# A transformer block on one core: an earlier start of the tensor engine, and instruction order set by hand dependencies

## The chip, the cores and the metric

The kernel runs on one core of one Trainium2 chip. The metric is device time in microseconds (us), as a median over runs. All runs quoted are of one core, and each run lists the mean clock granted to the tensor engine.

The engines go by the profile's names. PE is TensorE (matmuls), PEld its weight loads, DVE is VectorE, ACT is ScalarE, POOL is GpSimd and SP is SyncE. Two words need care. "The head" is the start of the kernel, up to the first q matmuls; "head 1" is `b_head` of chunk 1, the output projection described below. To evict is to copy a result out of PE's accumulator, which frees it for the next matmuls.

## The reference

The block has a pre-layernorm mixer and a gated MLP, S = 2048 rows, D = 1024. Cut to what matters:

```python
x = A_x
h  = x + A(layernorm(x))      # qkv = x @ wqkv; 32 heads of 32; each row attends to 8 rows,
                              # 0, 2, ..., 14 rows back (softmax over 8 logits); then @ wo
h2 = h + B(layernorm(h))      # z = gelu(x @ w_in); z1, z2 = halves of z; z2 = layernorm(z2)
                              # g = w_sp @ z2 + b_sp; (z1 * g) @ w_out
```

## The kernel before

The rows are worked in four chunks of 512. For each chunk there are four kinds of work, and they overlap across chunks:

1. `qkv(c)`: layernorm of x, transposes, then 192 matmuls on PE, evicted by ACT.
2. `attention(c)`: products and sums on DVE, about 80 us per chunk. For each of the 8 window positions `w`, DVE makes `part`, and four small PE matmuls write the logits `L`. After the eighth, softmax: DVE takes the maximum, ACT the exp, DVE the normalized `attn`. PE then spreads `attn` over the heads (`pb`), ACT evicts it (`AB`), and DVE makes the output `oT`.
3. `b_head(c)`: `oT @ wo` on PE, evicted by ACT (`hb`, `hnc`), then layernorm (`hnc` normalized by ACT).
4. `b_z2(c)`, `b_z1(c)`: the MLP's input matmuls, evicted by ACT with gelu (`u`, `z1s`).

```python
for i in range(NT):                       # layernorm of x, tile by tile
    xt = xts[i]
    st = l1.tile([P, 2, 6], FP32, name="bnst", tag="bnst")
    V.bn_stats(st[:, 0, :], xt[:, 0:512])
    V.bn_stats(st[:, 1, :], xt[:, 512:1024])
    V.bn_aggr(mv1[:, i, :], st[:])
    ...                                    # sqrt on ACT, reciprocal and normalize on DVE
    if c < 2:
        transpose_tile(...)                # 8 PE transposes, eviction by ACT
    ...
# attention(c)
for w in range(W_WIN):
    ...                                    # DVE: prod, t1_, t2_, part
    with tc.high_priority():
        for sq in range(4):
            T.matmul(L[32 * sq:32 * sq + 32, w, :], E32, part[:, sq * P:(sq + 1) * P], ...)
...
with tc.high_priority():
    A.activation(e, Ls, ACTF.Exp, scale=SCALE)
...
# program order
qkv(0); qkv(1); attention(0); qkv(2); b_head(0); attention(1); qkv(3); ...; b_head(1)
# then per chunk: b_z2(c), b_head(c+1) for c>0, b_z1(c), attention(c+2)
```

Each engine runs its instructions in the order that the build fixed (the traces of the changed kernel and of e4, two builds with the same order, agree in it on PE, DVE, ACT and POOL). A scheduler of the build works that order out from the program, its priorities and its own estimate of time. A "NoSync" dependency is there to change only this order, without a semaphore (a signal for which an engine waits).

## Time and profile before

| | |
|---|---|
| time | 773.97 us, median of 5 (773.35 to 774.67) |
| span of the profiled run | 772.2 us |
| PE busy | 742.4 us, 96% |
| first q matmul | 15.08 us |
| PE time lost after that | about 26 us (sum of what matmul starts lie further apart than usual), nearly all before 360 us |

From the profile page, the busy time of the engines (us, share of the span, instructions):

```profile
PE 742.4 (96%) x3704; PEld 379.9 (49%) x3704; DVE 439.6 (57%) x452; ACT 234.8 (30%) x304; POOL 20.1 (3%) x31
```

PE is the engine that bounds the kernel, so only moments when PE waits or runs slowly matter. The view of waits for PE names them. Its columns are: who waited, for whom, us in total, number of waits, the longest.

```profile
PE tpa L115 <- DVE xn L149: 9.8, 1, 9.8
PE L L229 <- DVE part L226: 4.8, 9, 2.0
PE acc L359 <- ACT u L361: 4.2, 1, 4.2
PE pb L253 <- DVE attn L245: 2.6, 3, 1.0
```

The first row is the start. The second is logits waiting for DVE's `part`. The third is a z2 matmul that finds no free accumulator, because ACT has not evicted one with gelu. The fourth is `pb` waiting for softmax.

The timeline of PE at the start (columns: start us, length us, engine, line, what; xN merges N instructions; in brackets, idle time before and what ended it):

```profile
9.83 4.15 PE L115 MATMUL tpa<-csb,xn 128*128 128x128 bf16 x32 [9.83 <-DVE xn L149]
15.08 5.21 PE L192 MATMUL acc<-xnT,wq 128*128 128x512 bf16 x14 [1.10 <-ACT xnT L116]
20.57 1.47 PE L192 MATMUL acc<-xnT,wq 128*128 128x512 bf16 x6
```

Fourteen q matmuls take 5.21 us, while six a little later take 1.47 us. Single starts show 0.425 us from one to the next for the first ten and 0.216 us after that: the array runs at half clock until about 19.2 us. The clock row of the page does not show it. It reads 9 (90% or more) from the first slice, because the first clock record of the trace, at 19.21 us, is the release itself.

The timeline of ACT around the 4.2 us wait:

```profile
245.02 4.62 ACT L328 ACTIVATE hnc<-hb,l2nb,l2rstd 128x1024 bf16<-128x1024 bf16 x4
249.66 1.28 ACT L239 ACT_TABLE_LOAD   x1
250.95 1.06 ACT L239 ACTIVATE scq<-scq 128x1024 bf16<-128x1024 f32 x1
252.02 1.28 ACT L361 ACT_TABLE_LOAD   x1
253.32 1.02 ACT L361 ACTIVATE u<-acc 128x1024 bf16<-128x1024 f32 x1
```

PE needs the gelu that starts at 253.32. Ahead of it in ACT's fixed order stand four normalizes (4.62 us) and exp of chunk 2 with a table load on each side (3.66 us together). The windows view gives what the wait does to the clock. Its columns are: window, length, then busy us (instructions) by engine, PEclk (1.00 is full), DMA share and GB/s.

```profile
237.00:250.00 13.00, 12.80 (x76) 6.38 (x75) 11.24 (x15) 12.82 (x15) 1.76 (x2) 1.00 0.37 122
250.00:262.00 12.00, 7.06 (x36) 3.87 (x34) 7.21 (x5) 9.43 (x13) 0.00 (x0) 0.72 0.58 135
```

A mean clock of 0.72 over 12 us is about 6.7 us at half clock (12 x 0.28 / 0.5). The clock record in the trace file has 6.83 us of it, from 254.73 us on.

### The profile page before, as it was taken

What the parts mean: (1) busy time and instruction counts of PE and PEld (TensorE: products, weight loads), DVE (VectorE), ACT (ScalarE), POOL (GpSimd) and SP (SyncE); (2) the same over time, 40 slices, a digit from 0 to 9 for tenths busy, and PEclk for the clock granted to TensorE, in tenths of its full rate; (3) what the DMA queues carried; (4) which work ended last, traced back from release to release, by engine and by line L of the source; (5) the groups of instructions that cost most, each with busy time, mean ns of one, the idle gap of its engine ahead of it and who ended that gap; (6) DMA issues with size and microseconds to landing.
All of it is one profiled execution on the core that took longest, in us unless ns stands there. A gap on an engine that the chain in (4) does not pass through costs nothing.

```text
span 772.2 us, 8881 instructions
## 1 busy us (share of the span) xinstructions
PE 742.4 (96%) x3704; PEld 379.9 (49%) x3704; DVE 439.6 (57%) x452; ACT 234.8 (30%) x304; POOL 20.1 (3%) x31
## 2 busy tenths in 40 slices
PE   4999999999999799999999999999999999999997
PEld 2666666546644444444545444444444444444443
DVE  6769799989998799979736020222222222212221
ACT  3522442256248845676551462000000000000000
POOL 0000000000000000000003000000000000000000
PEclk9999999999999899999999999999999999999999
DMA  9934364164884333145036957616211621020001
GB/s 330 340 132 97 124 180 138 56 225 112 291 304 165 66 134 115 41 178 124 14 141 250 276 191 215 190 31 175 71 42 42 178 68 42 28 81 28 1 21 62
DMA packets 104904, 102.24 MB, mean 132 GB/s; under 512 B 59232, under 2 KB 83200, under 8 KB 104736
## 3 DMA queue, kind: packets, MB, share of 16 engines
q1 hardware_dynamic: 98736, 75.52, 31.7%
q0 software_dynamic: 6128, 26.15, 9.8%
q8 instruction: 29, 0.48, 0.3%
q14 instruction: 11, 0.09, 0.0%
HBM read 55.19 MB, written 32.83 MB: 114 GB/s over the span
## 4 chain that ended last, share of the span: by engine, by line
PE 66%; DVE 23%; ACT 5%; issue 4%; DMA 1%; SPq 0%; DVEq 0%; ACTq 0%
PE acc L465 25%; PE acc L482 12%; PE acc L389 9%; PE acc L359 8%; PE acc L192 7%; DVE oT L264 5%; DVE prod L263 5%; DVE prod L220 4%; PE acc L303 4%; DVE scq L222 3%; DVE scq L224 2%; ACT hnc L328 1%; DVE part L226 1%; PE acc L490 1%; ACT AB L254 1%
## 5 line engine op out<-in xcount | busy, mean ns | idle before, releaser
L465 PE MATMUL acc<-wspT,z2sb 128*128 128x512 bf16 x896 | 194.0, 379 | 0.0
L465 PEld LDWEIGHTS <-z2sb 128*128 128x128 bf16 x896 | 87.7, 98 | 105.7
L468 DVE TENSOR_TENSOR g<-acc,bB 128x1024 bf16<-128x1024 f32 x28 | 34.3, 1225 | 159.7 <-PE acc L465 134.5
L359 PE MATMUL acc<-win,hnT 128*128 128x512 bf16 (+1 forms) x512 | 101.9, 358 | 4.2 <-ACT u L361 4.2
L389 PE MATMUL acc<-hnT,win 128*128 128x512 bf16 x448 | 98.8, 379 | 1.1 <-ACT z1s L392 1.1
L220 DVE TENSOR_TENSOR prod<-qT,kT 128x4096 bf16<-128x4096 bf16 x32 | 73.1, 2285 | 5.4 <-ACT kT L196 5.3
L359 PEld LDWEIGHTS <-hnT 128*128 128x128 bf16 x512 | 49.9, 99 | 50.8 <-issue 5.8
L389 PEld LDWEIGHTS <-win 128*128 128x128 bf16 x448 | 43.5, 98 | 52.1 <-issue 1.3
L482 PEld LDWEIGHTS <-zg 128*128 128x128 bf16 x420 | 41.1, 98 | 49.6
L263 DVE TENSOR_TENSOR prod<-vT,AB 128x4096 bf16<-128x4096 bf16 x28 | 64.1, 2291 | 1.4
L264 DVE TENSOR_TENSOR oT<-oT,prod 128x4096 bf16<-128x4096 bf16 x28 | 64.2, 2292 | 0.9
L192 PE MATMUL acc<-xnT,wq 128*128 128x512 bf16 x256 | 60.1, 389 | 2.0 <-ACT xnT L116 1.1
L199 ACT CAST stg<-acc 128x1024 bf16<-128x1024 f32 x36 | 36.2, 1013 | 79.9 <-PE acc L192 79.8
L303 PE MATMUL acc<-wo_sb,oT 128*128 128x512 bf16 x256 | 59.5, 379 | 0.0
L484 DVE TENSOR_TENSOR ot<-acc,hr 128x1024 bf16<-128x1024 f32 x15 | 18.4, 1224 | 69.4 <-PE acc L482 69.4
L192 PE MATMUL acc<-xnT,wv 128*128 128x512 bf16 x256 | 57.7, 380 | 0.0
L192 PE MATMUL acc<-xnT,wk 128*128 128x512 bf16 x256 | 56.8, 380 | 0.0
L482 PE MATMUL acc<-wout_a,zg 128*128 128x512 bf16 x240 | 54.2, 379 | 0.0
L192 PEld LDWEIGHTS <-wq 128*128 128x128 bf16 x256 | 36.1, 145 | 21.1 <-issue 4.8
L192 PEld LDWEIGHTS <-wk 128*128 128x128 bf16 x256 | 36.5, 144 | 18.2
L192 PEld LDWEIGHTS <-wv 128*128 128x128 bf16 x256 | 36.1, 144 | 17.5
L392 ACT ACTIVATE z1s<-acc 128x1024 bf16<-128x1024 f32 x28 | 28.4, 1025 | 42.6 <-PE acc L389 35.3
(97 smaller groups left out, 536.7 us busy)
## 6 DMA issues: line engine op xcount, KB each, us to landing
qkv_d<-stg SPq DMA_DIRECT2D x36, 256.0 KB, 2.9
z_d<-z1s SPq DMA_DIRECT2D x28, 256.0 KB, 2.9
z1c<-z_d SPq DMA_DIRECT2D x28, 256.0 KB, 2.7
z_d<-u SPq DMA_DIRECT2D x12, 448.0 KB, 3.6
z2sb<-z_d POOLq DMA_DIRECT2D x12, 448.0 KB, 8.5
xt<-in_A_x_dram SPq DMA_DIRECT2D x16, 256.0 KB, 9.7
xr<-in_A_x_dram SPq DMA_DIRECT2D x16, 256.0 KB, 2.8
h_d<-hb SPq DMA_DIRECT2D x16, 256.0 KB, 2.7
```

Source lines behind the costliest of these rows:

```text
L192: T.matmul(acc[:, j, :], wv[:, kt, dl, :], xnT[c][:, kt, :], start=(kt == 0), stop=(kt == KT - 1))
L199: A.copy(stg[:], acc[:])
L220: V.tensor_tensor(prod[:], qT[:], kT[:, :, o:o + CH], op=ALU.mult)
L263: V.tensor_tensor(prod[:], vT[:, :, o:o + CH], abb, op=ALU.mult)
L264: V.tensor_tensor(oT[:], oT[:], prod[:], op=ALU.add)
L303: T.matmul(acc[:, nh, :], oT[:, dl, il * P:(il + 1) * P], wo_sb[:, dl, nh * CH:(nh + 1) * CH], start=(last and dl == 0), stop=(dl == DLO - 1))
L359: T.matmul(accf[:, n0:n1], hnT[:, il, kt, :], wt[:, kt, n0:n1], start=(kt == 0), stop=(kt == KT - 1))
L389: T.matmul(acc[:, j, :].rearrange("p (a b) -> p a b", a=TPC), wt[:, kt, f0 * P:(f0 + 1) * P], hnT[:, :, kt, :], start=(kt == 0), stop=(kt ...
L392: A.activation(z1s[:], acc[:], ACTF.Gelu_apprx_tanh)
L465: T.matmul(acc[:, j, :], z2sb[a][:, f * P:(f + 1) * P], wspT[:, a, :], start=(a == 0), stop=(a == NT - 1))
L468: V.tensor_tensor(g1[:], acc[:], bB[:, c * CH:(c + 1) * CH].unsqueeze(1).to_broadcast([P, 2, CH]), op=ALU.add)
L482: T.matmul(acc[:, nh, :], zg[:, f, il * P:(il + 1) * P], wt[:, f0, nh * CH:(nh + 1) * CH], start=(f == 0), stop=(f == NF - 1))
```

## The change

The change has four parts.

1. **An earlier start.** The four x tiles of chunk 0 are requested first, on two queues. wq comes in eight pieces and is used as they come. The statistics of tile 3 move from DVE to ACT. The diff also takes the square roots of chunks 1 to 3 once per chunk instead of once per tile, evicts the transposes of tile 2 by DVE, and loads the table for the square root ahead.
2. **A warm clock.** Eighteen dummy matmuls on zeros keep PE busy from 1 us on, and ten more stand between and behind the transposes.
3. **Placement of logits** (`LATE`). For chunks 1 to 3, the first logits matmul of each window position may not stand before a named matmul in PE's order, so that PE does not stop for `part`.
4. **Placement of exp.** Exp of chunk 2 may not stand before a named gelu in ACT's order, the first one of the third row tile of z2 of chunk 0.

The diff, cut to its core:

```diff
+NWARM = 18
-    dma(csb[:], consts_d.ap()[:, :])
+    dma_w(csb[:], consts_d.ap()[:, :])
+    warm = cpool.tile([P, CH], BF16, name="warm")
+    V.memset(warm[:], 0.0)
 ...
+    wps = ps_att.tile([P, CH], FP32, name="wps", tag="L")
+    for _ in range(NWARM):
+        T.matmul(wps[:], warm[:, 0:P], warm[:], start=True, stop=True)
+    for i in (0, 3, 1, 2):
+        xts[i] = l1.tile([P, D], BF16, name="xt", tag="x2k", bufs=8)
+        (dma if i < 2 else A.dma_start)(xts[i][:], x2d[i * P:(i + 1) * P, :])
 ...
+    for kt in range(KT):
+        dma(wsb[0][:, kt, :], wq_view[:, kt, 0:D])
 ...
+    def stats_act(i):                      # tile 3: sums by two ACT passes
+        A.activation(jk[:], xts[i][:], ACTF.Identity, accum_out=sm[:, 0:1])
+        A.activation(jk[:], xts[i][:], ACTF.Square, accum_out=sm[:, 1:2])
 ...
+    def xpose(i, xn):
+        ... 8 transposes ...
+        for d in range(4 if i == 2 else 2):
+            T.matmul(wps[:], ident, xn[:, (d % 2) * CH:(d % 2 + 1) * CH], start=True, stop=True)
 ...                                        # q of chunk 0: four accumulators, kt outermost
+    LATE = {(1, 0): ('qkv', 2, 2, 0, 2), (1, 1): ('qkv', 2, 2, 2, 5), ... 24 entries ...}
 ...
+                    if sq == 0 and LATE.get((c, w)) in mms:
+                        tc.add_manual_dep(lg.ins, mms[LATE[c, w]].ins.name, <NoSync>, ...)
 ...
+        if c == 2:
+            tc.add_manual_dep(ex.ins, gelu[0, 2, 0].ins.name, <NoSync>,
+                              reason="exp of chunk 2 behind three gelu")
```

## The prediction

> **What bounds it now.** The tensor engine. The page has PE busy 742.4 of 772.2 us; the timeline shows back-to-back 512-column matmuls starting every 0.216 us, and that from 360 us on there is hardly a gap. The change touches only the first 350 us, so I count the time PE loses there (start-to-start distance above the normal one, read off the PE timeline):
> - Head: the first q matmul starts at 15.08 us, and its first ten run at 0.425 us each, about 2.2 us lost. The page's clock row does not show this (its records begin later). The Trainium skill ("TensorE: Matmul & The Clock Gate", Part 1) says the array clock is halved by default and released after some 3.4 us of sustained work; this trace agrees (fast from about 19.2 us).
> - Logits of chunks 1 to 3 waiting for VectorE's `part` (PE's waits): 2.1 us at 134, 1.2 at 215.5, 0.7 at 302, and some ten of 0.15 to 0.35: about 5.5 in sum.
> - At 249.9 us: 4.4 us waiting for ScalarE's gelu `u`. The ACT timeline shows why: four `hnc` (4.6 us), then exp of chunk 2 between two table loads of 1.28 us each, ahead of the gelu. The clock record then drops to half, and matmuls run at 0.425 us until 261: 2.3 us more, plus a 1.1 us wait for `attn`.
> - Left untouched: chunk 0's logits (2.4), `attn`, `stg` and `z1s` waits (4.5), the end (about 4).
>
> **What the change does.**
> - Head: x tiles are requested first and on two queues, wq comes in eight pieces used kt-first, one tile's statistics (about 1.6 us of VectorE) move to ScalarE (two 1.0 us passes). Tile 1 was waited for 1.0 us, until 6.06. The last normalize, at 12.9 now, should end near 10.3; transposes and eviction follow in about 2 us: first q matmul near 12.3 (gain 2 to 3.5). Eighteen dummy matmuls warm the clock meanwhile (gain 2.2); they cost nothing, PE being idle. Estimated from durations in this trace: 5.0 us, all critical, since PE has work from then on.
> - Logits placed some 5 to 9 matmuls (1 to 2 us) later for chunks 1 and 2: gain 2.2 + 1.4. VectorE continues meanwhile; three `part` buffers allow it.
> - Exp of chunk 2 behind three gelus: the gelu can follow `hnc` at 249.7, so the stall shrinks from 4.4 to about 1 us and the clock stays up: gain about 6. Exp comes some 5 us later, and attention of chunk 2 with it. That is off the critical path: oT of chunk 3 ends at 382 and is used at 399.4, a slack of 17 us, of which some 9 to 12 is consumed. Chunk 3's logits move some 8 us in the PE queue to match: gain 1.4.
>
> Sum: 5.0 + 3.6 + 6.0 + 1.4 = 16.0 us.
>
> **Prediction:** 758.0 us, 80% range 753.5 to 763.5. It sits near the 2% line (758.5): faster 0.53, same 0.46, slower 0.01.
>
> **What would show it.** Timeline: first q matmul at 11.5 to 13.2 us, at 0.216 us pitch from the start. PE's waits: `part` under 1.5 us in sum; the wait for `u` near 250 about 1 us or less, and no half-clock stretch after it. The order on ACT: gelu, gelu, gelu, exp. PE idle before the `wo` matmuls of chunk 3: none. PE busy time unchanged but for the dummies, and everything after 360 us only shifted.
>
> **What would make it wrong.** The clock falls again in the sparse stretch between dummies and q matmuls (minus 2). wq pieces or the x tiles land late. PE, now ahead, meets waits of VectorE elsewhere (oT of chunk 1 has only about 5 us slack; `attn`): the logits gain merely moves. ScalarE's deferred exp with its two table loads stalls a later gelu.

## The result, and the profile after

The changed kernel takes 760.52 us (median of 8, 759.62 to 761.81), against 773.55 us for the kernel before (median of 15). The ratio is 0.9835, 95% interval 0.9824 to 0.9846. Here and below, a ratio is the mean time of one kernel's fast runs over that of the other's in the same rounds, so it is not quite the ratio of the medians. The kernel is 1.65% faster: inside the predicted range, and inside 2%.

The eight runs fall into two groups: four at a mean clock of 1.000 take 759.62 to 760.02 us, and four at 0.997 or 0.998 take 761.01 to 761.81. The profiled run is of the first group (760.02), and that of the kernel before is a long one (774.33). So differences of about 1 us between medians of different kernels below can come from how many runs lost some clock; where that matters, runs at 1.000 are compared.

From the page of the changed kernel, the busy times, and then its view of PE's waits (columns as above):

```profile
PE 744.2 (98%) x3732; PEld 379.9 (50%) x3732; DVE 437.7 (58%) x445; ACT 236.3 (31%) x301; POOL 20.7 (3%) x32
```

```profile
PE L L288 <- DVE part L285: 3.3, 4, 2.2
PE pb L320 <- DVE attn L312: 2.7, 3, 1.0
PE tpa L170 <- DVE xn L162: 1.7, 1, 1.7
```

PE is busy 98% of a shorter span. The wait for gelu is gone from the list. The wait for `part` is not: 3.3 us remain in four waits, and the longest has grown from 2.0 to 2.2 us. It now sits elsewhere. The PE timeline of the start, and of the place where it sits:

```profile
11.81 0.61 PE L170 MATMUL tpa<-csb,xn 128*128 128x128 bf16 x8
13.30 7.10 PE L240 MATMUL acc<-xnT,wq 128*128 128x512 bf16 x32
...
209.28 2.75 PE L370 MATMUL acc<-wo_sb,oT 128*128 128x512 bf16 x12
214.20 0.24 PE L288 MATMUL L<-part,csb 128*32 128x128 bf16 x4 [2.17 <-DVE part L285]
```

The q matmuls start at 13.30 us at full speed: 32 in 7.10 us. At 214.20 us PE has waited 2.17 us for the first logits of chunk 2.

The ACT timeline of the changed kernel, and then its windows view where the kernel before had a clock of 0.72 (columns as above):

```profile
237.82 4.62 ACT L395 ACTIVATE hnc<-hb,l2nb,l2rstd 128x1024 bf16<-128x1024 bf16 x4
242.36 1.68 ACT L435 ACTIVATE junk<-u 128x1792 bf16<-128x1792 bf16 x1
244.03 1.00 ACT L428 ACTIVATE u<-acc 128x1024 bf16<-128x1024 f32 x1
245.03 0.79 ACT L428 ACTIVATE u<-acc 128x768 bf16<-128x768 f32 x1
245.81 1.01 ACT L428 ACTIVATE u<-acc 128x1024 bf16<-128x1024 f32 x1
248.22 1.06 ACT L302 ACTIVATE scq<-scq 128x1024 bf16<-128x1024 f32 x1
```

```profile
250.00:262.00 12.00, 11.03 (x80) 6.30 (x79) 10.14 (x7) 11.88 (x17) 0.00 (x0) 1.00 0.48 88
```

The three gelus (244.03, 245.03, 245.81) stand ahead of exp, and the clock is full. Exp is not late, though: it starts at 248.22 us, while before it started at 250.95.

To see where each us was won, I took the start of named matmuls from the two traces. The lead is by how much the changed kernel is ahead of the kernel before at that matmul:

| matmul | before, us | changed, us | lead, us |
|---|---|---|---|
| first q of chunk 0 | 15.08 | 13.30 | 1.78 |
| first v of chunk 0 | 46.94 | 43.30 | 3.64 |
| first matmul of head 1 | 215.03 | 208.85 | 6.18 |
| first logits of chunk 2 | 216.89 | 214.20 | 2.69 |
| first z2 of chunk 0 | 233.07 | 228.01 | 5.07 |
| first z2 of chunk 1 | 292.88 | 280.92 | 11.97 |
| first spatial matmul | 477.26 | 463.71 | 13.55 |
| end of span | 772.18 | 758.24 | 13.94 |

The lead falls between the third row and the fifth. A lead gained by PE was lost again at the logits of chunk 2, which DVE had ready only 2.69 us earlier than before.

### The profile page after: what moved, and what is told of

It is laid out like the page before. It is cut to its first block, busy times and chain, and to the rows that moved or that the text cites. A ratio compares the mean times of both kernels' runs of the same rounds, so it can differ in the third digit from the quotient of the medians.

```text
span 758.2 us, 8920 instructions
## 1 busy us (share of the span) xinstructions
PE 744.2 (98%) x3732; PEld 379.9 (50%) x3732; DVE 437.7 (58%) x445; ACT 236.3 (31%) x301; POOL 20.7 (3%) x32
## 4 chain that ended last, share of the span: by engine, by line
PE 63%; DVE 28%; ACT 4%; issue 4%; DMA 1%; DVEq 0%; ACTq 0%
PE acc L532 26%; PE acc L549 12%; PE acc L456 7%; PE acc L426 7%; DVE oT L331 6%; DVE prod L330 6%; PE acc L248 5%; DVE prod L279 5%; DVE scq L281 4%; PE acc L370 3%; DVE scq L283 2%; DVE part L285 1%; PE acc L240 1%; DVE oT L327 1%; PE acc L557 1%
## 5 line engine op out<-in xcount | busy, mean ns | idle before, releaser
L426 PE MATMUL acc<-win,hnT 128*128 128x512 bf16 (+1 forms) x512 | 98.9, 353 | 0.0
L248 PE MATMUL acc<-xnT,wq 128*128 128x512 bf16 x224 | 50.9, 380 | 0.0
L549 PE MATMUL acc<-wout_b,zg 128*128 128x512 bf16 x180 | 41.3, 379 | 0.0
```

The lines of the kernel that those rows point to most:

```text
L248: mms['qkv', c, xi, dl, kt] = T.matmul(acc[:, j, :], wv[:, kt, dl, :], xnT[c][:, kt, :], start=(kt == 0), stop=(kt == KT - 1))
L426: mms['z2', c, il, hf, kt, n0] = T.matmul(accf[:, n0:n1], hnT[:, il, kt, :], wt[:, kt, n0:n1], start=(kt == 0), stop=(kt == KT - 1))
L549: T.matmul(acc[:, nh, :], zg[:, f, il * P:(il + 1) * P], wt[:, f0, nh * CH:(nh + 1) * CH], start=(f == 0), stop=(f == NF - 1))
```

## The experiments

The comparison of instruction orders raised the first question. With the exp dependency and all eight placements of chunk 2 removed, the build gives the same instructions in the same order, on all engines, as the changed kernel. The traces (after, and e4 below) agree: PE 3732, DVE 445, ACT 301 and POOL 32 instructions, none at another place.

So part 4 and a third of part 3 change nothing in the presence of the rest. Two theories were set against each other. *Shared effect*: the reorder on ACT that removes the stall near 250 us follows from the placement of chunk 1's logits already, and the direct gain of that placement is partly lost at chunk 2. *Own shares*: each part brings what the prediction gave it.

### e1: the head alone

```diff
-    LATE = {(1, 0): ('qkv', 2, 2, 0, 2), ...}
+    LATE = {}
-        if c == 2:
+        if False:
             tc.add_manual_dep(ex.ins, gelu[0, 2, 0].ins.name, ...)
```

> The changed kernel without its placement table and without the exp dependency: only the new head is left. Head theory (both theories): every milestone of the before kernel from the k projection on comes 3.65 us earlier and nothing else changes; the 4.4 us stall near 246 us and the half-clock stretch are still there. About 770.0 us (ratio 0.995).

Measured: 770.5 us, ratio 0.9966 (0.9952 to 0.9981). The lead is 3.06 us at v of chunk 0 and 3.07 at the first spatial matmul: nothing else is gained. It is 0.6 us less than in the changed kernel, of which 0.5 us is a longer wait of PE at the transposes of chunk 1, near 25.1 us. The PE waits show the old stall unchanged:

```profile
PE L L288 <- DVE part L285: 4.8, 9, 2.0
PE acc L426 <- ACT u L428: 4.2, 1, 4.2
```

### e2: head and exp dependency, no placements

```diff
-    LATE = {(1, 0): ('qkv', 2, 2, 0, 2), ...}
+    LATE = {}
```

> Head plus the exp dependency, no placement table at all. Shared-effect theory: the ScalarE queue has exp of chunk 2 behind three gelus, as in the changed kernel, so the stall near 246 us and the half clock vanish: about 6.5 us below head only, 763.5 us. The 2.1 us wait of chunk 1's first logits (near 132 us) is back, but the 2.3 us wait of chunk 2's first logits (at 211.7 in the changed kernel) shrinks to about 1.2, so that PE arrives at z2 of chunk 0 within 1.2 us of the changed kernel. Rival (each part of the change brings its own share, as the prediction summed): also about 764, but PE would arrive at z2 of chunk 0 3.6 us later than in a kernel with the logits placed.

Measured: 764.46 us, ratio 0.9889 (0.9872 to 0.9906). The exp dependency by itself does bring the gelus ahead and is worth 6.5 us (lead 3.42 at z2 of chunk 0, 9.88 at z2 of chunk 1). Without placements, PE reaches z2 of chunk 0 with a lead of 3.42 us, 1.65 less than the changed kernel. That lies between what the two theories had said, 1.2 and 3.6.

### e3: head and the placements of chunk 1 alone

```diff
-    LATE = {(1, 0): ..., (2, 0): ..., (3, 0): ...}     # 24 entries
+    LATE = {(1, 0): ..., ..., (1, 7): ...}             # the 8 of chunk 1
-        if c == 2:
+        if False:
             tc.add_manual_dep(ex.ins, gelu[0, 2, 0].ins.name, ...)
```

> Head plus the eight placements of chunk 1's logits; no exp dependency, no placements for chunks 2 and 3. Shared-effect theory: the placements of chunk 1 alone already make the scheduler put exp of chunk 2 behind three gelus, so the stall near 246 us is gone without the exp dependency: about 762 us (only chunk 3's 1.6 us are missing against the changed kernel). Rival (own shares): the stall stays; head 3.65 and at most 2.2 us of logits, about 768 us.

Measured: 762.56 us, ratio 0.9857 (0.9838 to 0.9877). Own shares is refuted. Without any exp dependency, ACT's order has exp behind three gelus, and between z2 of chunk 0 and z2 of chunk 1 this kernel gains 6.90 us (lead 3.77 to 10.67).

Its trace holds one thing more. After the same wait of 2.17 us at the logits of chunk 2, the clock fell to half for a moment. PE's timeline of e3, the windows view of e3 there, and then PE's timeline of e4, which has the same wait and the same order there:

```profile
214.09 0.24 PE L288 MATMUL L<-part,csb 128*32 128x128 bf16 x4 [2.17 <-DVE part L285]
216.21 4.02 PE L370 MATMUL acc<-wo_sb,oT 128*128 128x512 bf16 x13
```

```profile
214.00:218.00 4.00, 3.91 (x15) 1.56 (x15) 3.97 (x4) 2.12 (x4) 0.00 (x0) 0.61 1.05 403
```

```profile
214.04 0.24 PE L288 MATMUL L<-part,csb 128*32 128x128 bf16 x4 [2.17 <-DVE part L285]
215.52 2.97 PE L370 MATMUL acc<-wo_sb,oT 128*128 128x512 bf16 x13
```

The clock of e3 is 0.61 over these 4 us. Thirteen matmuls take 4.02 us in e3 and 2.97 in e4. In all, PE's lead is 1.5 us smaller after this place than in e4. The wait thus costs its own length and, in some executions, half-clock time on top.

Why e3 and not e4? The trace files give a hint. In all 13 traces every change of the clock lies a whole number of 3.41 us after the first clock record (in e3: released at 6.69 us, halved at 214.91, which is 61 x 3.413 later). Count PE's idle time in periods of 3.41 us from there. Three periods inside the kernels were followed by a half clock: 3.16 us idle in the kernel before, 3.09 in e1, and 2.17 in e3, where the whole wait falls into one period (211.49 to 214.91). In e4 a period begins at 212.48 and cuts the same wait, so that neither part exceeds 1.56 us. The most idle period without a half clock has 1.96 us, in the changed kernel. Three cases are few for a rule, but they fit idle time being judged per period, so that the phase of the periods, and not only the length of a wait, decides.

### e4: the changed kernel without exp dependency and without chunk 2's placements

```diff
-    LATE = {(1, 0): ..., (2, 0): ..., (3, 0): ...}     # 24 entries
+    LATE = {...}                                       # 16: chunks 1 and 3
-        if c == 2:
+        if False:
             tc.add_manual_dep(ex.ins, gelu[0, 2, 0].ins.name, ...)
```

> The changed kernel without the exp dependency and without the eight placements of chunk 2: the instruction order of all five engines is the same as in the changed kernel. Shared-effect theory: the two parts do nothing beside the rest, 760.5 us as the changed kernel (ratio 0.983 to 0.985). Rival (own shares): 6 us of exp and 1.4 of chunk 2's logits are lost, about 768 us.

Measured: 760.53 us, ratio 0.9837 (0.9821 to 0.9854), as the changed kernel. The two parts are redundant beside the rest. As the two builds are the same program, e4 is at the same time a repeat of the changed kernel: the leads of the two traces below differ by 0.13 to 0.17 us, which gives an idea of their scatter. Its four runs split by clock as well (759.89 and 759.93 us at 1.000, 761.13 and 761.18 at 0.998). Against e3, the placements of chunk 3 bring about 1.4 us of lead: 13.68 against 10.82, less the 1.5 us of half clock in e3's trace.

| lead on the kernel before, us | changed | e1 | e2 | e3 | e4 |
|---|---|---|---|---|---|
| v of chunk 0 | 3.64 | 3.06 | 3.40 | 3.70 | 3.78 |
| first matmul of head 1 | 6.18 | 3.09 | 3.41 | 6.28 | 6.33 |
| logits of chunk 2 | 2.69 | 3.10 | 3.42 | 2.80 | 2.85 |
| z2 of chunk 0 | 5.07 | 3.11 | 3.42 | 3.77 | 5.23 |
| z2 of chunk 1 | 11.97 | 3.07 | 9.88 | 10.67 | 12.14 |
| first spatial matmul | 13.55 | 3.07 | 10.04 | 10.82 | 13.68 |

The third row tells of a side effect. Where chunk 1's logits are placed (changed, e3, e4), DVE reaches chunk 2 with 0.9 us less lead than it had at chunk 0. In e1 and e2 it does not. The ACT timelines suggest why, and e8 tests it.

### e5: no dummy matmuls

```diff
-NWARM = 18
+NWARM = 0
```

> The changed kernel without the eighteen dummy matmuls (the few dummies between the transposes stay). Clock theory: the first q matmul starts at the same 13.3 us, but the first eight to ten of 32 run at 0.425 us, so k of chunk 0 starts about 2 us later and the whole kernel takes about 762.5 us. Rival (the dummies between the transposes alone release the clock, or the start is bound by the landing of wq): k of chunk 0 within 0.5 us of the changed kernel, 760.5 to 761 us.

Measured: 762.17 us, ratio 0.985 (0.9835 to 0.9865), about 1.6 us slower than the changed kernel, or 2.3 us slower than its runs at a clock of 1.000, which all four runs have here. v of chunk 0 starts at 45.48 us instead of 43.30, which is 2.2 us later. The size was as expected, the place not:

```profile
9.06 1.03 PE L170 MATMUL tpa<-csb,xn 128*128 128x128 bf16 x8 [9.06 <-DVE xn L162]
12.45 1.06 PE L170 MATMUL tpa<-csb,xn 128*128 128x128 bf16 x8
14.09 0.61 PE L170 MATMUL tpa<-csb,xn 128*128 128x128 bf16 x8
15.57 1.70 PE L240 MATMUL acc<-xnT,wq 128*128 128x512 bf16 x7
```

The transposes and the dummies between them run cold. Eight transposes take 1.06 us there and 0.61 once the clock is released near 14 us. The q matmuls then start 2.3 us late, but fast. The run keeps the ten dummies between the transposes, and cold ones cost more too (1.06 us for two instead of 0.59): what the change would lose with no dummies at all was not run. (In the traces of e5 to e10 some 65 of about 3,700 matmul records are missing; starts are used here, not counts.)

### e6: statistics of tile 3 on DVE

```diff
-    stats_act(3)
+    stats(V, 3)
```

> The changed kernel with tile 3's statistics back on VectorE. If VectorE's chain of four tiles bounds the start: the first q matmul comes 0.7 to 1.5 us later than 13.3 us. If the landing of the x tiles or of wq bounds it: within 0.3 us of 13.3. Only the head is to be compared, as orders further on change too.

Measured: first q matmul at 14.19 us instead of 13.30, 0.89 us later; 761.0 us, ratio 0.9839 (0.9822 to 0.9856). The move to ACT is worth 0.9 us of the head. DVE's chain over four tiles bounds the start in e6, but not in the changed kernel: the last normalize is 1.76 us later in e6 (12.09 instead of 10.33 us), the q matmul only 0.89. In the changed kernel it is PE that is late (DVE and PE there):

```profile
10.33 0.55 DVE L162 TENSOR_SCALAR xn<-xt,mv,rstd 128x1024 bf16<-128x1024 bf16 x1
11.38 0.59 PE L172 MATMUL wps<-xn,csb 128*128 128x512 bf16 x2
11.81 0.61 PE L170 MATMUL tpa<-csb,xn 128*128 128x128 bf16 x8
12.26 1.03 PE L172 MATMUL wps<-xn,csb 128*128 128x512 bf16 x4
```

The last normalize ends at 10.88 us, and its transposes start at 11.81. Until then PE is busy without a gap, from 9.17 us on, with the other transposes and the dummies between them. No run takes these dummies out, so it stays open how much of the 0.93 us they cost.

### e7: logits of chunks 2 and 3 placed later

```diff
-    LATE = {..., (2, 0): ('o', 1, 0, 2, 0), ..., (3, 0): ('z2', 1, 2, 1, 6, 512), ...}
+    LATE = {..., (2, 0): ('o', 1, 1, 2, 1), ..., (3, 0): ('z2', 1, 3, 0, 6, 0), ...}
```

> The changed kernel with chunk 2's logits 2.4 us and chunk 3's 3.1 us later in the TensorE queue than they stand there. Slack theory: the 2.3 us wait at 211.7 and the 0.7 us wait near 299 are only a matter of order, since TensorE has other work and oT of chunk 3 is done 7.3 us before it is used; both waits vanish and the kernel takes about 757.8 us (ratio 0.980). Rival (VectorE paces this stage as a whole): the time is lost again at pb of chunk 2, at pb of chunk 3 or before the wo matmuls of chunk 3, and the kernel stays within 0.7 us of 760.5.

Measured: 760.41 us, ratio 0.9827 (0.9813 to 0.9842): no gain (its two runs at a clock of 1.000 take 760.16 and 760.24 us). The wait at 211.7 us did vanish, and PE reached z2 of chunk 0 with a lead of 7.64 us instead of 5.07. Then two new waits took it back:

```profile
PE L L288 <- DVE part L285: 2.7, 2, 2.4
PE acc L426 <- ACT u L428: 1.6, 1, 1.6
```

The second is ACT, with its four normalizes again ahead of the gelu that PE needs (at 244.18 us). It held up the last logits of chunk 2 by 1.9 us, and softmax waits for those. The first is now nearly all the fifth logits of chunk 3, which waited from 319 us on. At this point "DVE paces the stage" and "one fixed order does not fit another" were both still possible.

### e8: exp of chunk 1 ahead of the last eviction of head 0

In the kernel before, exp of chunk 1 stood ahead of the last pair of evictions of `b_head(0)` in ACT's order. The placements of chunk 1 moved it behind one of them.

```diff
+        if c == 1:
+            tc.add_manual_dep(hbis[0, 3].ins, ex.ins.name, <NoSync>, ...)
```

> The changed kernel with exp of chunk 1 ahead of the last eviction of head 0 in ScalarE's queue, as in the kernel before. If this order is what cost VectorE's chain 0.95 us (its lead falls from 3.64 to 2.69 us there): pb of chunk 1 and all logits of chunk 2 come about 0.95 us earlier, the wait at 211.7 shrinks from 2.3 to about 1.4 us, and the kernel takes about 759.6 us. Rival (the lead is lost elsewhere, or the gain is eaten at a later wait): 760.5 us.

Measured: 758.72 us, ratio 0.9804 (0.979 to 0.9819), on the 2% line. ACT's timeline, first of the changed kernel, then of e8:

```profile
164.22 1.02 ACT L381 ACTIVATE hb<-acc 128x1024 bf16<-128x1024 f32 x1 [2.04 <-PE acc L370]
165.24 1.05 ACT L302 ACTIVATE scq<-scq 128x1024 bf16<-128x1024 f32 x1
```

```profile
164.11 1.06 ACT L303 ACTIVATE scq<-scq 128x1024 bf16<-128x1024 f32 x1 [2.09 <-DVE scq L300]
165.07 1.01 ACT L386 ACTIVATE hb<-acc 128x1024 bf16<-128x1024 f32 x1
```

Exp starts 1.1 us earlier. The first logits of chunk 2 now have a lead of 3.84 us instead of 2.69. This order is what cost DVE 0.95 us in the changed kernel; undone, it beats the changed kernel by 1.8 us in the medians and 1.3 us in the spans. The difference is the clock: none of e8's four runs (758.65 to 758.78 us) fell below 0.999. PE still waits 1.46 us for the first logits of chunk 2.

### e9 and e10: orders fitted to each other

e9 adds to e8: three of head 1's four normalizes behind two gelus on ACT, logits of chunk 2 1.75 us later and of chunk 3 2.5 us later. e10 adds later `pb` for chunks 2 and 3, and puts chunk 3's logits 3.6 us later instead of 2.5. Both tables, and that of e11, also name places for chunk 0's logits; in e11's trace these stand behind as many other matmuls as in the changed kernel, so the entries moved nothing.

```diff
-    LATE = {..., (2, 0): ('o', 1, 0, 2, 0), ...}      # it stood behind ('o', 1, 0, 6, 0) in e8
+    LATE = {..., (2, 0): ('o', 1, 1, 1, 1), ...}      # and so on for chunks 2 and 3
+    PBLATE = {2: ('z1', 0, 0, 0, 6), 3: ('z1', 1, 6, 0, 3)}   # e10 only: first pb behind a named matmul
+                if (c, il, hf) == (0, 1, 1):
+                    for k in (1, 2, 3):
+                        tc.add_manual_dep(hncs[1, k].ins, gelu[c, il, hf].ins.name, <NoSync>, ...)
```

> Exp of chunk 1 first (as e8), three of head 1's four normalizes behind two gelus in ScalarE's queue, and chunk 2's logits 1.75 us, chunk 3's 2.5 us later in the TensorE queue. If the shifted logits of e7 failed because TensorE then ran into ScalarE (a 1.75 us wait for a gelu at 242 us) and so the last logits of chunk 2 came 1.9 us late: with the gelus ahead both the 1.6 us wait for chunk 2's first logits and the gelu wait are gone, TensorE reaches z1 of chunk 0 about 1.6 us earlier than in e8, and the kernel takes about 757 us (ratio 0.978). Rival (VectorE's chain paces this stage): the wait moves on to pb of chunk 2 or to chunk 3's logits, and it stays at 758.7 us.

> As e9, with the first pb matmuls of chunks 2 and 3 placed later too (2.85 and 4.5 us of matmuls) and chunk 3's logits 3.6 us later. If the two waits for attn (1.1 and 0.9 us) are a matter of order as well, another 2 us: about 755.5 us. Rival: VectorE's chain, lengthened by the later pb, ends after TensorE needs oT of chunk 3, and a new wait opens before the wo matmuls of chunk 3: 757 us or worse.

Measured: e9 759.04 us, ratio 0.9821 (0.9806 to 0.9837); e10 759.44 us, ratio 0.982 (0.9805 to 0.9836). Neither median is below e8's; at a clock of 1.000 e10's two runs take 758.22 and 758.33 us, 0.4 us less than e8. The gelu wait of e7 is gone, and PE reaches the first matmul of head 2 with a lead of about 16 us, against 12.8 in the changed kernel and 14.1 in e8. But near 318 us about 2.5 us are lost in both, at the fifth logits of chunk 3. The PE and DVE timelines of e10 there:

```profile
320.72 0.24 PE L291 MATMUL L<-part,csb 128*32 128x128 bf16 x4 [2.48 <-DVE part L288]
```

```profile
317.62 2.71 DVE L458 TENSOR_SCALAR u<-u,l3mean,l3rstd 128x1792 bf16<-128x1792 bf16 x4
320.25 0.41 DVE L288 TENSOR_TENSOR part<-scq 128x512 bf16<-128x512 bf16 x1
```

DVE scales `u` (four passes, 2.71 us) just before the fifth `part`. In the changed kernel the same scaling stands behind the fifth `part`, and the placements of chunk 3 allow for it there. The later placements had moved it by one position.

### e11: e10 with the fifth to eighth logits of chunk 3 later by 2.6 us

```diff
-    LATE = {..., (3, 4): ('o', 2, 3, 4, 1), ...}
+    LATE = {..., (3, 4): ('z1', 1, 0, 0, 5), ...}      # and (3, 5) to (3, 7) likewise
-    PBLATE = {2: ('z1', 0, 0, 0, 6), 3: ('z1', 1, 6, 0, 3)}
+    PBLATE = {2: ('z1', 0, 0, 0, 6), 3: ('z1', 1, 6, 1, 7)}
```

> As e10, with chunk 3's logits from the fifth on 2.6 us later still, and its first pb likewise. In e7, e9 and e10 the fifth logits of chunk 3 waited 2.5 us, because VectorE's order there has the 2.7 us scaling of u ahead of their part, while in the changed kernel it stands behind it. If that is the whole of the new wait, it goes and the kernel takes about 757 us, 2.5 us less than e10 and about 1.5 less than e8. Rival (TensorE and VectorE are tied over the whole stage): the 2.5 us come back before pb or the wo matmuls of chunk 3, 759 us.

Measured: 755.77 us (755.58 to 755.92), ratio 0.9768 (0.9755 to 0.9782). The output is correct. Among PE's waits, only these of any size are left besides the start and the end:

```profile
PE pb L327 <- DVE attn L319: 1.2, 2, 0.9
PE acc L377 <- DMA xr<-in_A_x_dram: 0.5, 1, 0.5
PE L L291 <- DVE part L288: 0.4, 1, 0.4
```

All five runs have a clock of 1.000. Against e10 the span is 2.6 us shorter (754.0 instead of 756.6), as expected; the medians differ by 3.7 us because three of e10's five runs lost some clock (0.997 to 0.998). The wait for `part` fell from 3.3 us in the changed kernel to 0.4 us. PE reaches the first `wo` of head 3 at 381.57 us, 4.3 us earlier than in the changed kernel, without a wait. So DVE did not pace this stage up to here: the waits were a matter of fixed order on three engines. But no slack is left. DVE ends oT of chunk 3 at 381.52 us, 0.05 us before PE reads it; it was 17.1 us ahead in the kernel before, and 7.35 in the changed kernel. A further gain of PE before this place would run into DVE. This version beats both kernels. What e11 adds to e8 was not timed part by part, so which of it is needed stays open.

## Why the prediction was right or wrong

The forecast of 758.0 us with 753.5 to 763.5 held: 760.52 us. The spans give 13.94 us gained (leads up to the spatial stage: 13.55), the timed medians 13.0, against 16.0 predicted; the profiled run of the kernel before is 0.8 us above its median, that of the changed kernel 0.5 us below. That the total held is in part luck: one term lost 2.2 us, the head 1.4, and the exp dependency, which the largest term rests on, changed nothing in this kernel. By terms of its sum:

| term | predicted, us | measured lead gained, us |
|---|---|---|
| head | 5.0 | 3.64 |
| logits of chunks 1 and 2 | 3.6 | 1.43 (5.07 - 3.64) |
| stall at 249.9 and its clock | 6.0 | 6.90 (11.97 - 5.07) |
| logits of chunk 3 | 1.4 | 1.58 (13.55 - 11.97) |

- **Head: right in kind, 1.4 us too large.** "The last normalize, at 12.9 now, should end near 10.3": it started at 10.33 and ended at 10.88. "First q matmul near 12.3" became 13.30, just outside the 11.5 to 13.2 that was to show it. The sum had no time for the ten dummies between the transposes: the last normalize was done as forecast, but its transposes waited 0.93 us for PE (see e6). ACT's copies run back to back until 12.67 us too, so which of the two set the start was not tested. The clock part was right in size: 1.86 us of lead between first q and first v, and 2.2 us in e5.
- **Logits of chunks 1 and 2: the step that failed.** "Logits placed some 5 to 9 matmuls (1 to 2 us) later for chunks 1 and 2: gain 2.2 + 1.4" treated the waits as independent. Chunk 1's wait did vanish, and its term held (2.54 us, 6.18 - 3.64). Chunk 2's term, 1.4 predicted, became a loss of 1.11 us (5.07 - 6.18). PE, 2.5 us further ahead by then, stood at the first logits of chunk 2 for 2.33 us instead of 1.22 (distance between starts beyond the usual one). The prediction named this under what would make it wrong ("the logits gain merely moves") but did not subtract it. A part of the loss is a side effect that it did not see: the placements of chunk 1 also moved exp of chunk 1 on ACT and so set DVE back by 0.95 us. With that undone (e8) the loss is 0.41 us (6.42 - 6.83). Chunk 2's placements turned out to change nothing: the scheduler placed those logits later by itself (e4).
- **Stall at 249.9: right mechanism and size, but credited to the wrong part of the change.** Gelus ahead of exp did end the stall and the half clock. The dependency on exp would have been enough (e2, 6.5 us), but in the changed kernel the placements of chunk 1 already bring the same order (e3), and removing the dependency costs nothing (e4).
- **"Exp comes some 5 us later": wrong.** It starts 2.7 us earlier. The gelus pass for the most part while DVE is still preparing exp's input. Of the slack of oT of chunk 3, some 9.7 us were consumed, as said (9 to 12): it is done at 378.5 us and used at 385.85. The figure holds by luck, as exp was not late: oT came 3.85 us earlier and PE 13.55.
- **"`part` under 1.5 us in sum": wrong.** It is 3.3 us, of which 2.2 is the moved wait.
- **Clock after the stall: right.** No half-clock stretch is left at 250 us.
- **"The clock falls again in the sparse stretch": did not happen.** The 32 q matmuls ran at full rate from the first.

## What to carry to other kernels

When each engine has a fixed order, a wait removed early moves the engine ahead of its partners, and it stops at the next place where the order assumed the old lead. Follow the lead from milestone to milestone through both traces instead of adding up the waits, and refit later placements after each gain (e7 gained nothing on the changed kernel, e9 and e10 next to nothing on e8; e11 gained 4.8 us on the changed kernel).

A dependency that only sets order can be redundant, or do its work on an engine that it does not name. Compare the built orders with and without it before giving it credit. Here the exp dependency and eight of the 24 placements changed no instruction's place beside the rest.

## What the Trainium skill lacked or had wrong

- "TensorE: Matmul & The Clock Gate", Part 1, gives an idle time of about one window (some 3.4 us) before the clock is halved. In e3 an idle time of 2.17 us was followed by a mean clock of 0.61 over 4 us, and in e4 the same wait was not. How much idle time within one window is enough is not given; here 2.17 us or more was followed by half clock (three cases), and up to 1.96 us never was (13 traces).
- The same page's figure for the release (about 3.4 us of sustained work, give or take) agrees roughly with the dense dummies here: in the changed kernel the first starts at 1.19 us, and the release is recorded at 5.78 us, 4.6 us later. In the eleven traces with these dummies it comes 3.1 to 5.5 us after the first. In the kernel before it came 9.4 us after the first transpose, and 4.1 us after the first q matmul (15.08 to 19.21 us).
- "ScalarE: Activation LUTs", What ACT_TABLE_LOAD costs, counts a load of 1283 ns and a drain of about 1380 ns for a switch of table set. The load is 1.28 us here too, but exp starts at 250.95 us, right at the end of the load that began at 249.66, and that load began right behind the work before it (245.02 + 4.62 = 249.64). No drain is seen at this switch, nor at the one back to gelu (252.02 us).
- No page says that the clock row of the profile page used here starts with the first clock record, so that a cold start reads as full clock: the page of the kernel before shows 9 in its first slice, while the first ten q matmuls ran at half rate.
